# Seven block products for batch 1's second stage, and a ring of three places in the first two batches

## The chip, the cores and the metric

The kernel runs on one core of a Trainium2 chip. The metric is the device time of one execution in microseconds (us). The core has five engines with queues of their own: TensorE (PE) multiplies, VectorE (DVE) and ScalarE (ACT) work on tiles and empty PSUM, GpSimd (POOL) works on tiles in SBUF and issues transfers, SyncE (SP) issues transfers. The transfers of all queues run on the same 16 DMA engines.

## The reference

Eight batches, eight heads, 576 positions, head size 64. Attention looks back over a window of 128 positions with a bias that falls with the distance; its output is read as 4608 tokens of 512 numbers. They go through a layer that takes the largest of three products, and through an output product.

```python
scores = scale * np.matmul(q, k.transpose(0, 1, 3, 2))
mask = (rel >= 0) & (rel < window)
scores = np.where(mask, scores + bias[None], -1000000000.0)
...
attn = attn / (np.sum(attn, axis=-1, keepdims=True) + 1e-09)
x = np.matmul(attn, v)  # as (4608, 512)
h = np.maximum(np.maximum(x @ w1, x @ w2), x @ w3)   # (4608, 768)
out = h @ w_out                                      # (4608, 512)
```

## The kernel before

**Two stages a batch.** Each of the eight batches (`b`) has an attention part, 18 steps, and a part of two matmul stages. While the stages of batch `b` run, the attention steps of batch `b + 1` stand between their matmuls. The first stage has nine groups (`g`): three hidden parts `p` of 256 features times the three matrices w1, w2, w3. The second stage has two groups, for the output's features. Everything is kept transposed, so a group is a 2 × 2 block product: the weights of a group are four blocks e0 to e3, the activations four blocks by half of the features and half of the positions (288 columns). Every number is held as a high and a low part in the fp32r format, and one block product over 128 rows is three matmuls (low × high, high × low, high × high).

**Plain and seven products.** Batches 0 and 1 (`PB = 2`) run both stages plainly: `plain` (L763 holds the matmuls) makes four results of a group, each the sum of two block products. Batches 2 to 7 use `unit` (matmuls at L815): seven block products of sums and differences of the blocks (Strassen's scheme in Winograd's form). One of a first-stage group's seven is six matmuls, one of a second-stage group's is nine; a plain result is 12 in the first stage and 18 in the second. The seventh product of a group (k = 6) runs three places later, among the next group's. `factors_x` makes the seven factors of the activations, `factors_h` those of the hidden part: subtractions at L606 (`sub`), and cuts into high and low at L602 (ACT) and L603 (DVE). `plain_x` and `plain_h` make the four plain halves. Plain results leave PSUM at L774 (ACT) and L777 (DVE, the maximum), or at L703 for the output. Those of `unit` leave at L832 (ACT) and L705 to L722 (DVE). Three PSUM banks serve all of them in turn.

**Weights.** Batch 0 prepares the weights itself: `preparing` takes a group through four steps, `exponents` (L165 on DVE, for the last three groups L169 and L170 on ACT), `convert` (L176 or L180, then L185, all on DVE) with a store to `plain_keep` (L315), and two times `part`, which cuts blocks into high and low (L199 ACT, L202 DVE), stores them to `keep` (L212) and asks for the raw weights of the next but one group (`fetch`, L151). Raw weights have two slots. Each plain product of batch 0 takes one step. The seven block products need sums and differences of the weights' blocks as well: `more_sums` reads the plain blocks back (`load_sums`, L224, two groups at a time into the slots of the raw weights), POOL makes the sums (L194), `split_sums` cuts them (L199, L202), `store_sums` stores them to `keep` (L243, L244). Groups 0 to 8 are weights of the first stage, 9 to 11 of the second, which stay in the tile `ow`. The list of `more_sums` goes by `now`, a count of 77 for each batch, 63 of them for the first stage; a plain product of the first stage is 1.75 of it.

**The ring.** First-stage weights stand in a ring of two places of seven blocks. `stream` loads a group from `keep` in two pieces through POOL's queue (L351 in batch 1, L356 later) when `ahead` says that the place is free. A plain group uses four of a place's seven blocks.

```python
def ahead(n, a):
    ...
    i = ringed[a].index(n)
    return i < RING or (ringed[a][i - RING], 6 if a else 3) in used
```

**What sets the order.** The events of attention and products are sorted by a step number written out at the end of the kernel (`at`). This is the order of the program. The framework's planner may then change the order on an engine: by its own costs, it lets an instruction that is ready pass one that is not, earlier ones of the program first. From batch 2 on PE's order is kept as it is written, as is that of a few others (`keep_in_program_order`). At run time each engine and each queue works its list in order.

Of the kernel before, what the change touches and what calls it, by code (L numbers as in the profile page):

```python
# [27 lines left out]
RING = 2  # L28
# [8 lines left out]
def attention_maxout_kernel(  # L37
# [99 lines left out]
    ring = const.tile([P, RING, 7, 2, W], F32R, name="ring")  # L137
# [67 lines left out]

    def part(g, n):
        f = ring[:, g % RING] if g < 9 else ow[:, :, g - 9]
        k, e = (slice(5, 7), slice(2, 4)) if n else (slice(0, 5, 4), slice(0, 2))
        hi_lo(f[:, k, 0], f[:, k, 1], floats(g)[:, e])
        if g < 9:  # L210
            i, k = (3, slice(4, 7)) if n else (1, slice(0, 1))
            nc.sync.dma_start(keep[g][n][:, :i], f[:, k].bitcast(F32))  # L212
# [4 lines left out]
    def load_sums():  # L217
        nonlocal loaded
        r = raw_tile()
        for n in range(2):  # L220
            g = loaded
            loaded += 1
            ts[g] = t = r[:, 2 * DM * n:2 * DM * (n + 1)].rearrange("p (e w) -> p e w", e=4)
            nc.sync.dma_start(t.bitcast(F32), plain_keep[g])  # L224
            to_sum.extend((g, n, now + 8) for n in range(2))
# [21 lines left out]
    def more_sums():  # L247
        if loaded < NG and all(g in finished for g in range(loaded - 4, loaded - 2) if g >= 0):
            load_sums()
        if now < 63:  # L250
            return
        if to_split and now >= to_split[0][2] and (to_split[0][0] >= 9 or (9 + to_split[0][0], 1) in wts):
            g, a, _ = to_split.pop(0)
            split_sums(g, a)
            if a:
                if g < 9:
                    later(now + 3, store_sums, g)
                else:
                    finished.add(g)
        elif to_sum and now >= to_sum[0][2]:  # L260
            g, n, _ = to_sum.pop(0)
            sums(ts[g].bitcast(F32), n)
            if n:
                to_split.extend((g, a, max(now + 6, 77 * PB if a and g >= 9 else 0)) for a in range(2))
                to_split.sort(key=lambda x: x[2])

    def place(n, a):
        wts[n, a] = ring[:, ringed[a].index(n) % RING, 4 * a:7 - 3 * (1 - a)]
# [7 lines left out]
    def ahead(n, a):  # L276
        if (n, a) in SPARE:
            return begun == B and (n < LAST + 8 or made == B)
        i = ringed[a].index(n)
        return i < RING or (ringed[a][i - RING], 6 if a else 3) in used  # L280
# [60 lines left out]
    def stream():  # L341
        nonlocal streamed
        if streamed < len(stream_order) and prepared == 4 * NG and ahead(*stream_order[streamed]):
# [4 lines left out]
            if n < 9 * PB:  # L348
                place(n, a)
                e = 3 if a else 1  # L350
                nc.gpsimd.dma_start(wts[n, a][:, :e], keep[n % 9][a][:, :e])  # L351
                return
# [385 lines left out]
    def plain(b, v):  # L738
# [7 lines left out]
        j, i = divmod(r, 2)  # L746
        ps = ps_m.tile([P, 512], F32, name=f"ps_m{((PLAIN + 8) * b + v) % 3}")[:, :C]
        at = 9 * b + g
        if g < 9:
            if b == 0:  # L750
                weights(1.0, 4 * g_order.index(g) + 4)
            pairs = [
                (ring[:, at % RING, PLAIN_AT[h][i], a, kt * P:(kt + 1) * P], xs[b, h, j][:, c, kt])
# [24 lines left out]
        if w == 2:  # L778
            later(unit_of(b, v + 1), plain_h, b, p, (i, j))

    def unit(u):
# [6 lines left out]
        if n < 11 * PB or n >= 11 * B:  # L788
            return
# [33 lines left out]
        if b == PB and len(finished) < NG:  # L823
            more_sums()
# [49 lines left out]
    for b in range(PB):  # L874
        pace = (ready[b + 1] - when) / PLAIN
        for c in range(PLAIN + 8):
            if c == PLAIN:
                when = max(when, ready[b + 1])
                if b + 1 < PB:
                    at(when, plain_x, b + 1)  # L880
                else:
                    at(when, factors_x, b + 1, 77 * b + 63, 1.2)
            at(when, plain, b, c)
            when += pace if c < PLAIN else O_PACE * 14 / 8
# [71 lines left out]
```

## Time and profile before

| What | us |
|---|---|
| median of three runs | 757.75 |
| lowest and highest run | 757.32, 759.4 |
| profiled execution | 759.31 |
| its span, from the first to the last instruction | 757.6 |

The profile is one execution. Its rows give times from the start of the span. "Busy" is the time in which an engine had at least one instruction running; matmuls overlap, so a matmul's own duration is longer than the distance to the next one.

### The profile page before, as it was taken

The numbers are of one execution on the slowest core, as the hardware profiler recorded it, in microseconds if no ns is written. First come the engines' busy times: TensorE is split into PE (matmuls) and PEld (weight loads), VectorE is DVE, ScalarE is ACT, GpSimd is POOL, SyncE is SP. The second block draws the span as 40 slices with busy tenths as digits, with TensorE's granted clock in tenths as the row PEclk, the third lists the DMA queues.
The fourth block names the chain that finished last, engine by engine and source line by source line (L and its number), as shares of the span: only waits on it lengthen the run. The fifth ranks groups of instructions, "written<-read, shape, count | busy, mean of one in ns | idle before, by whom it ended". The sixth has DMA issues, their size and how long they took to land.

```text
span 757.6 us, 19290 instructions
## 1 busy us (share of the span) xinstructions
PE 736.8 (97%) x7216; PEld 676.0 (89%) x7221; DVE 516.2 (68%) x1617; ACT 482.4 (64%) x1597; POOL 235.9 (31%) x451
## 2 busy tenths in 40 slices
PE   7979999999999999999999999999999999999998
PEld 3448889998999999999999999999899999999998
DVE  4869977636559567794687657794777747683663
ACT  5775767666567767776766757676667767552342
POOL 4651214555555323222222123211222122333100
PEclk9999999999999999999999999999999999999999
DMA  7867999659999488864988479864988468789611
GB/s 250 302 234 262 326 334 336 214 199 288 308 330 386 146 271 305 280 209 153 329 295 288 135 245 306 304 217 144 300 283 276 166 221 285 269 252 367 235 65 63
DMA packets 57085, 192.81 MB, mean 254 GB/s; under 512 B 5792, under 2 KB 24480, under 8 KB 50464
## 3 DMA queue, kind: packets, MB, share of 16 engines
q0 software_dynamic: 20304, 108.54, 43.4%
q1 hardware_dynamic: 36400, 82.85, 31.3%
q8 instruction: 57, 0.93, 0.5%
q14 instruction: 36, 0.29, 0.1%
q10 hardware_dynamic: 288, 0.20, 0.1%
HBM read 156.95 MB, written 34.60 MB: 253 GB/s over the span
## 4 chain that ended last, share of the span: by engine, by line
PE 70%; DVE 10%; DMA 7%; POOL 5%; ACT 4%; issue 3%; SPq 0%; POOLq 0%; DVEq 0%; ACTq 0%
PE ps_m L815 45%; PE ps_m L763 11%; PE ps_s L420 4%; PE ps_x L555 4%; PE pt L488 4%; DMA ring<-keep 3%; DVE hs L603 2%; DMA hs<-in_w_all 2%; DVE hq L720 2%; DVE t L719 2%; POOL hs L194 2%; POOL pp L512 1%; POOL pp L508 1%; DMA keep<-hs 1%; DVE t L606 1%
## 5 line engine op out<-in xcount | busy, mean ns | idle before, releaser
L815 PE MATMUL ps_m<-xs,ring 128*128 128x288 f32 x2160 | 302.5, 297 | 1.8 <-DVE hq L722 1.3
L815 PEld LDWEIGHTS ps_m<-xs,ring 128*128 128x128 f32 x2160 | 290.1, 188 | 4.7 <-ACT t L832 3.1
L508 POOL TENSOR_SCALAR_AFFINE_SELECT pp<-pr 128x256 f32<-128x256 f32 x112 | 51.9, 463 | 278.3 <-ACT pr L492 152.9
L461 ACT ACTIVATE p<-s,st 128x128 f32<-128x128 f32 x288 | 114.6, 400 | 25.0 <-DVE st L449 20.8
L763 PE MATMUL ps_m<-xs,ring 128*128 128x288 f32 x864 | 123.1, 299 | 4.6 <-DMA ring<-keep 2.3
L763 PEld LDWEIGHTS ps_m<-xs,ring 128*128 128x128 f32 x864 | 116.3, 188 | 7.4 <-DMA ring<-keep 3.0
L832 ACT COPY t<-ps_m 128x288 f32<-128x288 f32 x196 | 76.8, 394 | 71.9 <-PE ps_m L815 69.9
L356 POOL DMA_DIRECT2D ring<-keep x103 | 55.5, 539 | 166.2 <-PE ps_m L815 155.6
L815 PE MATMUL ps_m<-hs,ow 128*128 128x288 f32 x756 | 105.7, 297 | 0.4
L815 PEld LDWEIGHTS ps_m<-hs,ow 128*128 128x128 f32 x756 | 100.9, 188 | 2.6 <-ACT t L832 1.2
L480 ACT ACTIVATE p<-p,st 128x128 f32<-128x128 f32 x252 | 84.8, 393 | 23.1 <-DVE st L468 23.1
L719 DVE TENSOR_TENSOR t<-ps_m,t 128x288 f32<-128x288 f32 x108 | 48.9, 453 | 43.6 <-PE ps_m L815 34.2
L449 DVE CUSTOM_DVE_ANT_0 s<-ps_s,bias 128x128 f32<-128x128 f32 x240 | 60.7, 285 | 11.1 <-POOL bias_t L111 4.6
L420 PE MATMUL ps_s<-qk 64*64 64x192 f32 (+1 forms) x1088 | 61.8, 319 | 1.5 <-DVE st L449 1.4
L602 ACT CAST hs<-hq 128x288 fp32r<-128x288 f32 x96 | 40.4, 432 | 34.3 <-DVE hq L720 17.8
L461 ACT ACTIVATION_READ_ACCUMULATOR p<-s,st 128x1 f32 x288 | 55.2, 192 | 0.0
L555 PE MATMUL ps_x<-pp,v 64*64 64x64 f32 (+3 forms) x1456 | 53.9, 276 | 0.0
L488 PE MATMUL pt<-plus,p 128*128 128x128 f32 x288 | 48.7, 287 | 3.6 <-POOL p L475 3.6
L555 PEld LDWEIGHTS ps_x<-pp,v 64*64 64x64 f32 x1456 | 42.3, 134 | 10.3 <-issue 9.2
L488 PEld LDWEIGHTS pt<-plus,p 128*128 128x128 f32 x288 | 30.5, 141 | 22.9 <-issue 12.9
L512 POOL TENSOR_SCALAR_AFFINE_SELECT pp<-pr 128x256 f32<-128x256 f32 (+1 forms) x112 | 50.3, 449 | 1.1
L589 DVE TENSOR_TENSOR xk<-ps_x,xk 128x256 f32<-128x256 f32 (+3 forms) x56 | 25.4, 454 | 36.8 <-ACT xk L588 36.8
(92 smaller groups left out, 954.4 us busy)
## 6 DMA issues: line engine op xcount, KB each, us to landing
ring<-keep POOLq DMA_DIRECT2D x51, 1024.0 KB, 7.3
ring<-keep POOLq DMA_DIRECT2D x61, 768.0 KB, 5.9
qk<-in_qk SPq DMA_DIRECT2D x31, 576.0 KB, 6.0
hs<-in_w_all SPq DMA_DIRECT2D x12, 1023.6 KB, 6.4
v<-in_v SPq DMA_DIRECT2D x32, 320.0 KB, 6.4
outT<-t SPq DMA_DIRECT2D x64, 144.0 KB, 1.8
keep<-ring SPq DMA_DIRECT2D x9, 768.0 KB, 6.0
plain<-hs SPq DMA_DIRECT2D x12, 512.0 KB, 4.2
```

Of the source, the lines that this page charges most:

```text
L420: pe(nc.tensor.matmul(ps[j][d:d + D, o:o + k1 - k0], lhsT=qkt[u][j * D:(j + 1) * D, 0, q0:q0 + D], rhs=qkt[u][j * D:(j + 1) * D, 1, k0:k1] ...
L449: nc.vector.tensor_tensor_reduce(out=x, in0=ps[j][:, P:2 * P], in1=below, scale=-0.125, scalar=3.0e38, op0=ALU.add, op1=ALU.min, accum_out ...
L461: nc.scalar.activation(p[:, j], x, AF.Exp, bias=st[:, 0, a, j:j + 1], scale=-1.0, accum_out=st[:, 1, a, j:j + 1])
L480: nc.scalar.activation(p[:, j], p[:, j], AF.Copy, scale=st[:, 2, a, j:j + 1])
L488: pe(nc.tensor.transpose(out=pt[:, a, j], in_=p[:, j], identity=ident))
L508: nc.gpsimd.affine_select(out=old, in_=src, pattern=[[-x, n] for x, n in pat], compare_op=ALU.is_gt, fill=0.0, base=0, channel_multiplier=1,)
L512: nc.gpsimd.affine_select(out=new, in_=low, pattern=pat, compare_op=ALU.is_ge, fill=0.0, base=0, channel_multiplier=-1,)
L555: pe(nc.tensor.matmul(x[j * D:(j + 1) * D, r, o:o + rhs.shape[1]], lhsT=vv[k, i, j * D:(j + 1) * D], rhs=rhs[k], start=start, stop=True, s ...
L719: nc.vector.tensor_tensor(out=s, in0=ps, in1=e, op=ALU.add)
L763: pe(nc.tensor.matmul(ps, lhsT=lt, rhs=rt, start=n == 0, stop=n == len(pairs) - 1, skip_group_check=True))
L815: pe(nc.tensor.matmul(part_of[n, {2: 0, 5: 0, 6: 0, 3: 1}.get(kk, kk)], lhsT=lt, rhs=rt, start=first, stop=i == len(pairs) - 1, skip_group ...
L832: nc.scalar.copy(out=e, in_=ps)
```

## The change

Batch 1's second stage goes through `unit` instead of `plain`, so the hidden part of batch 1 gets the seven factors, and the order of the four results of a group in batch 1 is that which `factors_h` expects. The ring becomes one row of 14 blocks; in batches 0 and 1 a group takes four of them, at one of three places, and later seven at one of two. `ahead` goes by the group three before instead of two before. The sums for the seven products must be done by batch 1's second stage, so the due times in `more_sums` are shorter, and a split and a sum may follow in one call.

```diff
-    ring = const.tile([P, RING, 7, 2, W], F32R, name="ring")
+    ring = const.tile([P, 7 * RING, 2, W], F32R, name="ring")
...
+    def plain_place(n):
+        return ring[:, 4 * (n % 3):4 * (n % 3) + 4]
...
     def part(g, n):
-        f = ring[:, g % RING] if g < 9 else ow[:, :, g - 9]
-        k, e = (slice(5, 7), slice(2, 4)) if n else (slice(0, 5, 4), slice(0, 2))
-        hi_lo(f[:, k, 0], f[:, k, 1], floats(g)[:, e])
+        e = slice(2 * n, 2 * n + 2)
         if g < 9:
-            i, k = (3, slice(4, 7)) if n else (1, slice(0, 1))
-            nc.sync.dma_start(keep[g][n][:, :i], f[:, k].bitcast(F32))
+            f = plain_place(g)
+            hi_lo(f[:, e, 0], f[:, e, 1], floats(g)[:, e])
+            k = slice(1, 4) if n else slice(0, 1)
+            nc.sync.dma_start(keep[g][n][:, :k.stop - k.start], f[:, k].bitcast(F32))
+        else:
+            f = ow[:, slice(5, 7) if n else slice(0, 5, 4), g - 9]
+            hi_lo(f[:, :, 0], f[:, :, 1], floats(g)[:, e])
...
-            to_sum.extend((g, n, now + 8) for n in range(2))
+            to_sum.extend((g, n, now + 7) for n in range(2))
...
-        if to_split and now >= to_split[0][2] and (to_split[0][0] >= 9 or (9 + to_split[0][0], 1) in wts):
+        if to_split and now >= to_split[0][2] and (to_split[0][0] >= 9 or streamed > 2 * to_split[0][0] + 1):
...
-                    later(now + 3, store_sums, g)
+                    later(now + 2, store_sums, g)
...
-        elif to_sum and now >= to_sum[0][2]:
+        if to_sum and now >= to_sum[0][2]:
...
-                to_split.extend((g, a, max(now + 6, 77 * PB if a and g >= 9 else 0)) for a in range(2))
+                to_split.extend((g, a, max(now + 4, 78 if a and g >= 9 else 0)) for a in range(2))
...
     def place(n, a):
-        wts[n, a] = ring[:, ringed[a].index(n) % RING, 4 * a:7 - 3 * (1 - a)]
+        k = 7 * (ringed[a].index(n) % RING)
+        wts[n, a] = ring[:, k + 4 * a:k + 7 - 3 * (1 - a)]
...
+        if n < 9 * PB:
+            return n < 3 or (n - 3, 3) in used
         i = ringed[a].index(n)
+        if i < 9 * PB + RING:
+            return all((x, 3) in used for x in range(i - 3, i - 1))
...
             if n < 9 * PB:
-                place(n, a)
-                e = 3 if a else 1
-                nc.gpsimd.dma_start(wts[n, a][:, :e], keep[n % 9][a][:, :e])
+                k = slice(1, 4) if a else slice(0, 1)
+                nc.gpsimd.dma_start(plain_place(n)[:, k], keep[n % 9][a][:, :k.stop - k.start])
                 return
...
-        j, i = divmod(r, 2)
+        j, i = ((0, 0), (0, 1), (1, 0), (1, 1))[r] if b < PB - 1 else ((1, 0), (0, 0), (1, 1), (0, 1))[r]
...
-        if w == 2:
+        if w == 2 and b < PB - 1:
             later(unit_of(b, v + 1), plain_h, b, p, (i, j))
+        elif w == 2:
+            factors_h(b, p, (i, j), unit_of(b, v + 1))
...
-        if n < 11 * PB or n >= 11 * B:
+        if n < 11 * PB - 2 or n >= 11 * B:
...
-        if b == PB and len(finished) < NG:
+        if len(finished) < NG:
             more_sums()
...
-            at(when, plain, b, c)
-            when += pace if c < PLAIN else O_PACE * 14 / 8
+            if c < PLAIN or b < PB - 1:
+                at(when, plain, b, c)
+                when += pace if c < PLAIN else O_PACE * 14 / 8
+        if b == PB - 1:
+            for u in range(77 * b + 63, 77 * b + 77):
+                at(when, unit, u)
+                when += O_PACE
```

## Rows read from the trace of the kernel before

**Rows 1.** The page, busy time, share and instructions of an engine.
```profile
PE 736.8 (97%) x7216; PEld 676.0 (89%) x7221; DVE 516.2 (68%) x1617; ACT 482.4 (64%) x1597; POOL 235.9 (31%) x451
```

**Rows 2.** Windows: stages of batches 0 and 1; length, busy by engine, clock, DMA.
```profile
core 0: us, PE busy (x) PEld busy (x) DVE busy (x) ACT busy (x) POOL busy (x), PEclk, DMA share, GB/s
58.64:139.36 80.72, 77.86 (x815) 71.67 (x815) 66.97 (x193) 54.48 (x171) 21.50 (x42) 0.98 0.89 319
139.36:161.03 21.67, 21.67 (x188) 20.86 (x185) 9.15 (x30) 12.84 (x43) 8.70 (x11) 1.00 0.52 174
161.03:238.13 77.10, 74.79 (x803) 70.62 (x802) 47.84 (x148) 50.17 (x165) 44.01 (x73) 1.00 0.93 306
238.13:260.56 22.43, 22.43 (x212) 21.62 (x210) 15.21 (x36) 15.61 (x47) 12.04 (x15) 1.00 0.65 232
```

**Rows 3.** Waits of PE, 58.64 to 260.56: us in total, times, longest.
```profile
PE ps_m L763 <- DMA ring<-keep: 2.3, 3, 1.4
PE ps_m L763 <- DVE hq L777: 1.9, 1, 1.9
PE ps_s L420 <- DVE st L449: 1.0, 1, 1.0
```

**Rows 4.** The chain of waits in batch 1: start, us, what.
```profile
169.47 8.81 DMA ring<-keep
...
195.10 9.44 DMA ring<-keep
...
206.07 8.15 DMA keep<-hs
214.28 5.02 DMA hs<-plain
...
222.61 7.58 DMA ring<-keep
```

**Rows 5.** The chain of waits in batch 0, 92 to 112.
```profile
93.35 7.07 DMA hs<-in_w_all
...
100.51 1.14 ACT hs L169
```

**Rows 6.** Windows: the stretch at the lower clock, columns as in rows 2.
```profile
108.93:112.35 3.42, 3.42 (x49) 2.56 (x47) 2.62 (x10) 3.30 (x11) 0.00 (x0) 0.50 0.98 397
```

**Rows 7.** Timeline of PE, batch 1's second stage, one of two such rows.
```profile
238.13 9.69 PE L763 MATMUL ps_m<-hs,ow 128*128 128x288 f32 x72
```

**Rows 8.** Lines L602, L603, L606, L705: duration ns min/median/max, first and last start.
```profile
L602 ACT CAST hs<-hq x96: 413/433/440, 76.5 to 740.5; 128x288 fp32r<-128x288 f32 x96
L603 DVE TENSOR_TENSOR hs<-hq,hs x96: 426/451/1079, 77.2 to 741.1; 128x288 fp32r<-128x288 f32 x96
L606 DVE TENSOR_TENSOR t<-hq,t x36: 445/451/455, 283.1 to 740.8; 128x288 f32<-128x288 f32 x36
L705 DVE TENSOR_TENSOR t<-ps_m,t x36: 441/457/459, 333.1 to 753.1; 128x288 f32<-128x288 f32 x36
```

**Rows 9.** Windows: batch 2's second stage, columns as in rows 2.
```profile
325.00:346.00 21.00, 20.94 (x198) 19.74 (x195) 16.90 (x51) 15.28 (x50) 3.32 (x7) 1.00 0.51 175
```

**Rows 10.** The sums and splits by line; last, L194 alone, windows added up.
```profile
L194 POOL TENSOR_TENSOR hs<-hs x48: 724/746/1417, 138.5 to 250.1; 128x256 f32<-128x256 f32 x48
...
L199 ACT CAST xs<-hs x18: 604/618/623, 147.3 to 232.2; 128x512 fp32r<-128x512 f32 x18
...
L202 DVE TENSOR_TENSOR hs<-hs,xs x18: 680/693/1249, 148.0 to 233.3; 128x512 fp32r<-128x512 f32 x18
...
161.00:238.00 77.00, 24.68 (x30) 1.00 0.93 305
238.00:260.50 22.50, 8.28 (x8) 1.00 0.65 234
```

**Rows 11.** Timeline of SP's issues in batch 0.
```profile
86.70 0.33 SPq L383 DMA_DIRECT2D qk<-in_qk  x1
87.14 0.43 SPq L315 DMA_DIRECT2D plain<-hs  x1
...
92.92 0.33 SPq L388 DMA_DIRECT2D v<-in_v  x1
93.35 0.38 SPq L151 DMA_DIRECT2D hs<-in_w_all  x1
```

More of the change, by code (lines that the diff above doesn't have):

```diff
@@ L752, in plain @@
             pairs = [
-                (ring[:, at % RING, PLAIN_AT[h][i], a, kt * P:(kt + 1) * P], xs[b, h, j][:, c, kt])
+                (plain_place(at)[:, (0, 3, 1, 2)[2 * h + i], a, kt * P:(kt + 1) * P], xs[b, h, j][:, c, kt])
                 for h in range(2) for kt in range(2) for a, c in ((0, 1), (1, 0), (0, 0))
```

## The prediction

> **What bounds the kernel now.** I read the page first: TensorE (PE) is busy 736.8 of 757.6 us [rows 1]. So time can come from fewer matmuls, from the 21 us in which PE is idle, or from a stretch at the lower clock. The stretches touched are batch 0 and batch 1, so I cut the span at their stages [rows 2]. Batch 0's first stage (58.64 to 139.36) holds 2.9 us of idle PE, batch 1's (161.03 to 238.13) 2.3 us, the two second stages none. The waits of PE name nearly all of that [rows 3]: three waits for a ring load (2.3 us together), one for VectorE's (DVE) maximum at L777 (1.9 us), one for a score (1.0 us).
>
> The chain of waits tells why the ring loads were late [rows 4]. The load issued at 169.47 took 8.81 us, the one at 195.10 took 9.44, the one at 222.61 7.58. With two places a group's load may start only when the group two before it is used up, so its whole lead is the four products of one group: (77.1 − 2.3) / 36 = 2.08 us each, 8.3 us. The DMA share there is 0.93 [rows 2], and no faster load is in sight.
>
> The wait for L777 comes from the preparation of weights in batch 0 [rows 5]: a load of raw weights issued at 93.35 lands 7.07 us later, ScalarE (ACT) has the exponents of that group next in its queue and starts them at 100.51, DVE's conversion waits for them, and the maximum that frees a PSUM bank stands behind the conversion on DVE. After that idle time the granted clock fell: 0.50 (1.2 GHz) from 108.93 to 112.35 with PE busy throughout [rows 6]. Half of 3.42 us, 1.7 us, is lost there, so this one late load cost 3.6 us.
>
> **The change part by part.** *Fewer block products.* Batch 1's second stage was two groups of four products of 18 matmuls, 144. It becomes two groups of seven of 9, 126 (the seventh of the last group runs among batch 2's first products, and is counted here). 72 such matmuls take 9.69 us [rows 7], 0.135 us each; 18 × 0.135 = **−2.4 us**. No matmul is added elsewhere, so I keep this as fixed.
>
> *Three places.* A place now comes free one group earlier, so a load in batch 1 has eight products, 16.6 us, before its use. The longest of the three took 9.44 [rows 4]; 7 us are left for a late issue. All three waits should go: **−2.3 us**, bounds −2.3 and 0. The loads keep their size and their number; one issue of some 0.55 us stands per half group, on the same POOL queue. The first three groups of batch 1 are now loaded within batch 0, into a second stage where DMA is busy 0.52 [rows 2]. The page DMA: Bandwidth & Descriptors of the Trainium skill (Anatomy of one DMA) gives 2.0 us plus bytes at 436 GB/s, an estimate of 3.8 us for these 768 KB. By that a lead of 8.3 us would be ample, the third place would bring nothing and the sum would be −2.4; the rows, twice as long, contradict it.
>
> *Batch 2's first two groups* still enter the ring when groups 16 and 17 of the plain places are used: the same products as before, nothing gained or lost.
>
> *Factors instead of plain halves.* Each of the three hidden parts now needs seven cuts instead of four and four subtractions. In all 9 more casts on ACT (0.433 us, 3.9 us), 9 more low parts (0.451) and 12 subtractions (0.451) on DVE, 9.5 us. The outputs: six DVE additions (0.457) come in, 2.7 us, and ACT keeps about eight copies [rows 8]. So DVE gets 12.2 us more, ACT 3.9. What hides it: DVE is busy 47.8 of 77.1 us in the first stage and 15.2 of 22.4 in the second [rows 2]. Some 5.9 us of it belongs to the second stage (3 low parts, 4 subtractions, 6 additions at 0.45). The nearest like stretch is batch 2's second stage, 325 to 346: the same seven products with the same factors of the next batch, DVE 16.9 of 21 us, PE 20.94 [rows 9]. That cover held, so I cost it at **0**. Bounds 0 and +3, half of the 5.9 us laid bare; a gain is excluded, since PE is not idle there.
>
> *Sums moved forward.* The twelve groups' sums (48 POOL instructions, 0.746 us median), their splits (ACT 0.618, DVE 0.693) and stores all have to end before batch 1's second stage. Working through the code's list by its due times: the pairs of loads were asked for at products 2, 11, 19 and 28 of batch 1 and are now at 1, 7, 15 and 23; the last splits, before in batch 2, are now at products 31 to 34. Work and bytes are the same, only packed. Does the last pair come in time? Before, the pair asked for at product 19 (161.0 + 19 × 2.14 = 201.7) was issued at 214.28, behind a store that took 8.15 us, and its load took 5.02 [rows 4], 17.6 us after asking (219.3). Now the last pair is asked for at 161.0 + 23 × 2.08 = 208.8, and so lands near 226.4. Its eight POOL sums at 0.87 (24.68 + 8.28 us for 30 + 8 of them [rows 10]) bring 233.3, the last split, cast and low part one after the other, about 2 us more: 235.3. The second stage begins at 238.13 − 2.3 = 235.8, and its second block product meets the last group's factors 15 matmuls later, near 237.8. The margin is 2.5 us: **0**, bounds 0 and +5 (one more block like the store's 8.15 us, less the margin and rounded). What queues behind a late load: on POOL the masks of the attention and the ring issues; on SP the stores and the loads of q, k and v. Before, SP stood still for the 8 us of that store without a wait of PE but the ring's [rows 3, 4].
>
> *POOL beside DVE.* The same instruction of POOL takes from 0.724 to 1.417 us, the DVE subtraction of the split 0.680 to 1.249 [rows 10]. The page GPSIMD Engine Reference of the Trainium skill (Key points) says that POOL shares its way into SBUF with DVE and suffers from DVE instructions with two inputs there; these rows agree. At 1.417 eight sums take 11.3 us instead of 6.9, and the margin of 2.5 us is gone: this is the third rival's mechanism.
>
> *Preparation moved forward.* Group n's parts used to wait for group n − 2's use, now n − 3's; in the order of the code each step comes three products earlier in batch 0. But the trace shows these steps held by the raw loads, whose slot has to be stored first, not by the ring. So they can hardly run earlier. What changes is SP's order. Before, a store waited behind a q,k load (86.70, 87.14) and the raw load behind a v load (92.92, 93.35) [rows 11]. By their places in the code both now go ahead, which I estimate at one to two us on the load that came late. Against it, the planner may now put exponents still further ahead of PSUM evictions. Bounds −3.6 (the stall and its clock go) and +3.6 (one more of the kind). Both ends are equally far, so I take **0**.
>
> **Sum.** −2.4 − 2.3 + 0 + 0 + 0 = −4.7 us. The profiled execution took 759.31 us with a span of 757.6, 0.2% above the median of the runs, 757.75. I take the difference off the median: **753.0 us**.
>
> **The rivals.**
> 1. *The preparation's stall goes too.* For it: SP's new order. Against: the raw loads themselves take 7 us in a stretch with DMA at 0.89 [rows 2]. −4.7 − 3.6: 749.4.
> 2. *The third place brings nothing*, since the DMA engines are full (0.93) and an earlier issue only makes each load slower. −2.4: 755.4. Against it: each load gets 8.3 us more of lead, and the stretch before has room (0.52).
> 3. *The last sums come late* and the second stage waits, with POOL slowed by DVE or SP blocked once more by 8 us: +2 to +5 on the forecast, 755 to 758. It decides from a delay of 2.5 us on.
> 4. *Slower:* exponents placed three products further ahead of evictions make ACT and DVE wait for raw loads that arrive when they always did, PE runs out of PSUM banks. Each such stall costs 1.9 + 1.7 us as seen once [rows 3, 6]. One gives 756.6; from two on (7.2 us) the change loses: 760.2. For it: DVE is the busiest there, 67.0 of 80.7 us. Against: the steps already ran later than their places in the code ask.
>
> **How the numbers follow.** Chances: forecast 0.42, rival 1 0.20, rival 2 0.10, rival 3 0.15, rival 4 0.13. A measurement of this kernel can tell some 0.3%, 2.3 us, from no change, so the border lies at 755.5. Faster: forecast, rival 1, half of rival 2 and a third of rival 3 less a bit for the unseen, 0.69. Slower: half of rival 4 and what mishaps I did not see, 0.11. Same: the rest, 0.20. The range reaches down past rival 1 (749.4, and one microsecond more if the score's wait [rows 3] goes as well) and up to rival 3's end and past one stall of rival 4: 748.4 to 758.0. What is left out is two stalls, and less than 2 in 10.
>
> **What would show each step.** 126 instead of 144 matmuls on hidden and output weights in batch 1, and its two stages shorter by 2.4 us beside the waits. No PE wait for a ring load in batch 1, with the loads still 7 to 9 us long but issued a group ahead. DVE at about 0.8 in batch 1's second stage with PE without idle time. POOL's last sum some 2 us before that stage begins. In batch 0 one clock drop after one idle stretch, as before, or none (rival 1), or two (rival 4). I am wrong if PE idles at the head of batch 1's second stage, or if batch 0's first stage changes by more than 2 us.

## The result and the profile after

The changed kernel is slower, by about 1%: 768.04 us (median of 8 runs, 765.31 to 770.77) beside 760.79 us for the kernel before (8 runs on the same chip, 757.32 to 764.59). The ratio is 1.0098, 95% interval 1.0073 to 1.0124. The forecast was 753.0 us, with 748.4 to 758.0 as the range and 0.11 as the chance of slower. The profiled execution took 767.95 us, its span is 766.2.

The page of the changed kernel, for [rows 1]:

```profile
PE 739.0 (96%) x7198; PEld 675.9 (88%) x7203; DVE 525.8 (69%) x1644; ACT 483.8 (63%) x1606; POOL 234.7 (31%) x451
```

The 18 matmuls are gone (7216 to 7198), and yet PE is busy 2.2 us longer, part of it at half clock. DVE has 9.6 us more, ACT 1.4. Windows of the same stages, columns as in [rows 2]; the last line is both batch 1's second and batch 2's first stage, and two short windows follow in a second answer:

```profile
60.66:142.17 81.51, 77.70 (x815) 70.51 (x815) 67.43 (x193) 54.83 (x171) 23.57 (x44) 1.00 0.90 326
142.17:163.84 21.67, 21.67 (x188) 20.86 (x185) 10.83 (x31) 13.30 (x44) 14.16 (x17) 1.00 0.64 220
163.84:244.97 81.13, 76.03 (x803) 71.89 (x802) 55.03 (x162) 52.43 (x173) 45.23 (x74) 0.98 0.86 287
244.97:332.77 87.80, 84.60 (x837) 79.98 (x839) 59.53 (x200) 58.54 (x201) 20.21 (x45) 0.98 0.71 238
...
221.30:224.70 3.40, 3.20 (x15) 2.92 (x15) 3.40 (x12) 2.44 (x10) 1.48 (x3) 0.50 0.98 324
252.00:255.40 3.40, 3.40 (x16) 3.40 (x16) 2.30 (x4) 2.74 (x9) 0.00 (x0) 0.50 0.00 0
```

Batch 0, from the first line's start to the second's end, lasts as long as before within a microsecond (103.18 and 102.39 us). Batch 1's first stage takes 81.13 us instead of 77.10, with 5.1 us of idle PE instead of 2.3 and 3.4 us at half clock. Here DVE is busy 55.0 us instead of 47.8. Another idle stretch and another 3.4 us at half clock stand in the second stage. The 2.0 us by which the window begins later (60.66 against 58.64) arise in the first 22 us: PE waits 1.6 us for a load of q and k there, and the clock stands at 0.50 for 6.8 us instead of 3.4. They are no mark of the change: in the nine profiles of kernels with the changed kernel's batch 0, this point lies between 57.7 and 61.0, and the kernel before's among them. PE's waits of the changed kernel, for [rows 3]:

```profile
PE ps_m L773 <- DVE hq L787: 4.3, 3, 3.8
PE ps_m L827 <- ACT t L844: 3.1, 1, 3.1
PE ps_m L773 <- ACT hq L784: 1.3, 1, 1.3
```

No ring load is waited for in batch 1's first stage any more. What PE waits for are PSUM banks: DVE's maximum (L787), ACT's copies out of PSUM (L784, L844). The chain of waits of the changed kernel, for [rows 4], says who was late before 221:

```profile
189.94 7.00 DMA ring<-keep
...
197.34 3.91 DMA keep<-hs
...
201.68 5.86 DMA hs<-plain
207.54 0.95 POOL hs L194
...
211.00 5.85 DMA ring<-keep
...
221.08 0.38 DVE hq L787
```

One round trip: a ring load, the store of sums that may overwrite its source only after it (SP waits), the load of the next groups' blocks behind that store on SP's queue, the sums on POOL. The timeline shows what stood behind it, ACT first, then DVE:

```profile
213.65 0.62 ACT L199 CAST xs<-hs 128x512 fp32r<-128x512 f32 x1 [5.38 <-POOL hs L194]
214.18 0.43 ACT L612 CAST hs<-hq 128x288 fp32r<-128x288 f32 x1
...
214.63 0.80 DVE L613 TENSOR_TENSOR hs<-hq,hs 128x288 fp32r<-128x288 f32 x1 [4.58 <-ACT hs L612]
...
221.00 0.45 DVE L787 TENSOR_TENSOR hq<-ps_m,hq 128x288 f32<-128x288 f32 x1
```

A split of sums (L199) held ACT for 5.38 us. The cut of a hidden factor (L612) is next in ACT's list, and DVE waited 4.58 us for it. Then everything that had piled up ran first, until at 221.00 the maximum came for which PE had stood since 217.7. (L202, L613 and L616 are DVE's low parts and differences; in this pile of 6.4 us they were stretched by about 1.2 us, so the 4.58 us of waiting weigh more.)

### The profile page after: what moved, and what is told of

Its sections match the earlier page's. It is cut to its first block, busy times and chain, and to the rows that moved or that the text cites. A ratio compares the mean times of both kernels' runs of the same rounds, so it can differ in the third digit from the quotient of the medians.

```text
span 766.2 us, 19305 instructions
## 1 busy us (share of the span) xinstructions
PE 739.0 (96%) x7198; PEld 675.9 (88%) x7203; DVE 525.8 (69%) x1644; ACT 483.8 (63%) x1606; POOL 234.7 (31%) x451
## 4 chain that ended last, share of the span: by engine, by line
PE 68%; DVE 11%; DMA 8%; ACT 6%; POOL 3%; issue 3%; SPq 0%; POOLq 0%; DVEq 0%; ACTq 0%
PE ps_m L827 46%; PE ps_m L773 9%; DMA ring<-keep 4%; PE ps_s L430 4%; PE pt L498 4%; PE ps_x L565 4%; DVE hs L613 2%; ACT p L471 2%; DVE hq L730 2%; DVE t L729 2%; DMA qk<-in_qk 1%; POOL pp L522 1%; POOL p L485 1%; DMA keep<-hs 1%; ACT p L490 1%
## 5 line engine op out<-in xcount | busy, mean ns | idle before, releaser
L518 POOL TENSOR_SCALAR_AFFINE_SELECT pp<-pr 128x256 f32<-128x256 f32 x112 | 53.0, 474 | 291.7 <-ACT pr L502 160.1
L827 PE MATMUL ps_m<-hs,ow 128*128 128x288 f32 x882 | 124.9, 299 | 3.5 <-ACT t L844 3.1
L844 ACT COPY t<-ps_m 128x288 f32<-128x288 f32 x202 | 78.9, 393 | 72.9 <-PE ps_m L827 71.0
L827 PEld LDWEIGHTS ps_m<-hs,ow 128*128 128x128 f32 x882 | 119.4, 190 | 5.9 <-ACT t L844 4.5
L612 ACT CAST hs<-hq 128x288 fp32r<-128x288 f32 x96 | 40.2, 433 | 26.9 <-DVE hq L730 17.8
L522 POOL TENSOR_SCALAR_AFFINE_SELECT pp<-pr 128x256 f32<-128x256 f32 (+1 forms) x112 | 50.1, 448 | 1.1
```

The lines of the kernel that those rows point to most:

```text
L522: nc.gpsimd.affine_select(out=new, in_=low, pattern=pat, compare_op=ALU.is_ge, fill=0.0, base=0, channel_multiplier=-1,)
L827: pe(nc.tensor.matmul(part_of[n, {2: 0, 5: 0, 6: 0, 3: 1}.get(kk, kk)], lhsT=lt, rhs=rt, start=first, stop=i == len(pairs) - 1, skip_group ...
L844: nc.scalar.copy(out=e, in_=ps)
```

## The experiments

Three theories were put up. **Theory 1**: the sums, due earlier, make ACT and DVE stand behind late loads and late POOL sums. **Theory 2**: the factors' extra work on DVE and ACT starves PE of PSUM banks. **Theory 3**: the third place itself does harm. Each run is compared with the kernel before on its own chip.

### Three places alone

The change without its second stage and with the old due times:

```diff
-            to_sum.extend((g, n, now + 7) for n in range(2))
+            to_sum.extend((g, n, now + 8) for n in range(2))
...
-        if n < 11 * PB - 2 or n >= 11 * B:
+        if n < 11 * PB or n >= 11 * B:
```

> Three places of four blocks, but batch 1's second stage plain and the due times of the sums as in the kernel before. Theory 1 (the sums' earlier due times make ACT and DVE stand behind late POOL sums): the three ring waits of 2.3 us go and nothing else comes, ratio to the kernel before 0.995 to 0.998. Theory 2 (the 12 us more of DVE work for the seven factors are what starves PE of PSUM banks): the same, 0.995 to 0.998. Theory 3 (the third place itself harms, by earlier preparation in batch 0 or by earlier ring loads): 1.003 or more, with new idle stretches of PE in the two first stages.

Measured 757.28 us (12 runs), ratio **0.9956** (0.9931 to 0.9981): faster than both kernels, and theory 3 falls. Its windows (batch 1's first stage, then all up to the end of batch 2's first stage), and the shares of its chain of waits between 160 and 236:

```profile
163.03:237.04 74.01, 74.01 (x803) 70.55 (x801) 46.67 (x145) 49.66 (x165) 43.83 (x73) 1.00 0.94 318
237.04:322.25 85.21, 85.07 (x855) 80.70 (x856) 60.00 (x191) 59.51 (x202) 27.70 (x52) 1.00 0.74 251
```

```profile
by line: PE ps_m L773 78.2%; PE ps_x L565 8.5%; PE ps_s L430 7.2%; PE pt L498 6.2%
```

PE has no idle time in 74 us, no DMA is left in the chain, and the DMA share is still 0.94. ACT's splits wait for POOL's sums here too, 6.2 us in four pieces of at most 2.7, without a cost to PE.

### Three places and early sums

The same with the changed kernel's due times; the second stage stays plain.

> As e1, but with the changed kernel's due times of the sums (load to sum 7, sum to split 4, split to store 2, a split and a sum in one call); batch 1's second stage plain, no factors of the hidden part. Theory 1: the idle stretches of batch 1's first stage (3.8 and 1.3 us, and 1.7 us of clock) are there without any factor: 6.8 less 2.3 won, ratio 1.004 to 1.007. Theory 2: they are not there, 0.995 to 0.999.

Measured 760.78 us (12 runs), ratio 0.999 (0.9967 to 1.0014). The early sums alone cost 3.5 us (757.28 to 760.78): less than theory 1 expected, and the upper end of what theory 2 allowed. Its first stage in the windows, and ACT's waits in it:

```profile
162.47:240.70 78.23, 75.11 (x804) 70.68 (x801) 47.38 (x145) 48.48 (x161) 44.76 (x74) 1.00 0.92 297
```

```profile
ACT ow L199 <- POOL hs L194: 8.0, 2, 4.9
```

4.2 us more than with the old due times at nearly the same busy time of DVE and ACT: it isn't work but waiting. PE's waits show behind what:

```profile
PE ps_x L565 <- POOL pp L518: 1.3, 1, 1.3
PE ps_m L773 <- DVE hq L787: 1.2, 2, 0.6
PE ps_x L565 <- POOL pp L522: 0.7, 1, 0.7
```

Of the 3.1 us of idle PE, 2.0 stand before products that need the attention's masks (L518, L522): on POOL these came behind six sums in a row (211.3 to 216.6), after POOL had stood 6.0 us for the load they read. The other 1.2 us are maxima on DVE (at 233.8 and 236.3) behind a low part (L202) whose split ACT had held for 4.9 us. So late sums stop two lists, POOL's own and ACT's.

### No sums on POOL

The changed kernel without the 48 sums, so that what is cut and stored from batch 1 on are unsummed blocks.

```diff
-            sums(ts[g].bitcast(F32), n)
             if n:
```

> The changed kernel with the 48 sums on POOL left out (loads, splits and stores stay, so the seven products use plain blocks in place of sums). Theory 1: ACT's casts no longer wait for POOL, the idle stretches of batch 1's first stage go (5.1 us and 1.7 us of clock), the 3.1 us at the second stage stay: ratio to the kernel before about 1.001. Theory 2: no change from the changed kernel, 1.008 to 1.011.

Measured 764.16 us (10 runs), ratio 1.0057 (1.0033 to 1.0082). Less loss, but the stall stayed: between what the two theories expected (1.001; 1.008 to 1.011). In its profile, taken from the slowest of its runs (768.87), PE is idle 6.0 us at 213.3. ACT now waits for the transfers themselves:

```profile
ACT xs L611 <- DMA keep<-xs: 5.5, 1, 5.5
ACT xs L199 <- DMA hs<-plain: 4.8, 1, 4.8
```

The first is a cut that needs a slot whose sums are still on their way out, the second a split whose load is late. POOL's sums are one link of the round trip; without them the late transfers alone make a stall.

### A tile of its own for the fourth block

```diff
+            if n:
+                nc.sync.dma_start(last_keep[g], f[:, 3:4].bitcast(F32))
...
```

> The changed kernel, but the plain fourth block of a group is kept in a DRAM tile of its own, so that the store of the fourth sum does not wait on SP for the ring load that reads the plain fourth block from the same place. One more store and one more ring issue of 256 KB per group, the same bytes. Theory 1, with SP's waits for ring loads as the start of the chain: those waits of SP go, the sums' loads land some 4 us earlier against the products, the 3.8 us idle stretch shrinks below 1: 1.001 to 1.004. Theory 2: no change, 1.008 to 1.011. If the sums are late for another reason than that wait: no change either, with SP's waits gone.

Measured 767.95 us (6 runs), ratio 1.0095 (1.0062 to 1.0128): no gain, where theory 1 had 1.001 to 1.004. SP's waits for ring loads in batch 1 (28.0 us in the changed kernel) are gone, and SP waits for its own stores instead, in front of the next load:

```profile
SPq L233 <- DMA keep<-hs: 25.9, 8, 8.2
```

### Four cuts instead of seven factors

The factors behind batch 1's first stage are not formed; products 1, 2 and 6 of its second stage read the cuts of 0, 3 and 4. 12 differences and 9 cuts are left out.

```diff
     def factors_h(b, p, ij, when):
+        if b == PB - 1 and p < 3:
+            return four_h(b, p, ij, when)
```

> The changed kernel, but behind each three first-stage blocks of batch 1 the seven factors are not formed: only the four maxima are cut (as in the kernel before), and products 1, 2 and 6 read the cuts of products 0, 3 and 4, so the values of batch 1 are not the reference's. All matmuls, waits for weights, sums and due times stay; 12 differences and 9 cuts (about 9.5 us of VectorE, 3.9 us of ScalarE) are gone. Theory 2 (the factors' work starves TensorE of banks): the idle of 3.8 us near 217 and the one of 3.1 us in the second stage go, batch 1's first stage takes 76 to 78, the second about 20; ratio 0.994 to 1.000. Theory 1 (the sums, early and behind a long DMA round trip, stop ScalarE's queue): the first stage keeps an idle of 2 us or more and takes 79 to 81, only the second stage's idle goes; ratio 1.002 to 1.006.

Measured 763.55 us (11 runs), ratio 1.0043 (1.0017 to 1.0069), as theory 1 expected. PE's waits:

```profile
PE ps_m L800 <- DVE hq L814: 4.1, 2, 3.9
PE ps_m L854 <- ACT t L871: 1.4, 2, 1.2
```

The stall near 217 needs no factors: 3.9 us, as before. The one in the second stage falls from 3.1 to 1.2 us, and no clock drop follows it.

### Four cuts for the last third only

The same with `p == 2` in place of `p < 3`.

> As the run with four cuts, but only for the last third of batch 1's inner rows (p = 2), whose factors are formed at the seam of its two stages; the factors of p = 0 and 1 stay. Leaves out 4 differences and 3 cuts (3.2 us of VectorE, 1.3 of ScalarE) right before the second stage. If the second stage's idle of 3.1 us comes from those factors, it is under 1 us here and the second stage takes 20.5 to 21.5 with no clock drop behind it; the first stage keeps its idle near 217 under both theories. Ratio 1.002 to 1.006. If it comes from the next batch's factors instead, idle stays at 2.5 to 3 us and the ratio at 1.008 to 1.010.

Measured 765.18 us (11 runs), ratio 1.0067 (1.0041 to 1.0093). The second stage's idle was 2.2 us, between what the two readings expected, so the last third's factors look like a part of it. The first stage's long idle now stood at 195.9 (2.5 us) instead of 217.7.

### The next batch's factors later

```diff
-                    at(when, factors_x, b + 1, 77 * b + 63, 1.2)
+                    at(when, factors_x, b + 1, 77 * b + 68, 1.2)
```

> The changed kernel with the seven input factors of batch 2 begun five units later in batch 1's second stage (about 7 us), so that they don't stand among the last factors of batch 1; nothing is left out. If the idle of 3.1 us at 247.6 is VectorE's pile of both batches' factors, it falls under 1.5 us and the clock drop behind it goes: ratio 1.003 to 1.007. If the last factors of batch 1 alone do it, nothing changes there (1.008 to 1.011); if batch 2's first unit then waits for its factors, an idle of 1 to 3 us shows at the start of batch 2 instead.

Measured 765.23 us (11 runs), ratio 1.0048 (1.0026 to 1.0071). The time is in the expected range, but not for the reason given: the idle in the second stage was 2.6 us, hardly less; no clock drop followed it in the profile.

### No sums, and a tile of its own

Both links of the round trip out, all factors kept (unsummed blocks, as above).

> The changed kernel without the 48 sums on GpSimd (the folded weights stay plain sums' inputs, so the values from batch 1's second stage on are not the reference's) and with the fourth plain block in a tile of its own, so that SyncE's stores of sums don't wait for the ring's loads. Loads, splits and stores of the sums stay. Theory 1 (what stops ScalarE is a split that waits for its load and sum): with both links of the round trip out, the splits find their data there, the first stage has no idle over 1.5 us and takes 77 to 78; ratio 0.998 to 1.003. Theory 2 (factors): idle of 3 to 4 us near 217 stays; ratio 1.005 to 1.010.

Measured 760.34 us (11 runs), ratio 0.9995 (0.997 to 1.0019). The first stage takes 78.1 us, 2.3 us of it idle at 214.8, where theory 1 had under 1.5. Most of the loss is gone, not all.

### No sums, a tile of its own, and four cuts

> The changed kernel with both suspects out: four cuts instead of seven factors (12 differences and 9 cuts left out), no sums on GpSimd, and the fourth plain block in a tile of its own. The values from batch 1's second stage on are not the reference's; all matmuls, ring loads, splits and stores of sums stay. If these two causes are all of the loss, what is left is the run with three places alone (0.9956) less 18 matmuls (2.4 us of 761, 0.0032): ratio 0.990 to 0.995, first stage 74 to 75.5, second 20.1 to 20.6, no idle over 1 us. If something else in the change costs (the blocks' order in the first stage, the order of loads), ratio 0.997 to 1.002 with idle over 2 us somewhere in batch 1.

Measured 757.62 us (11 runs), ratio 0.9963 (0.9938 to 0.9989), between the two readings (0.990 to 0.995 and 0.997 to 1.002). Its windows:

```profile
166.58:241.88 75.30, 74.26 (x803) 70.57 (x802) 47.15 (x152) 51.04 (x169) 23.18 (x48) 1.00 0.93 306
241.88:325.34 83.46, 83.14 (x837) 78.47 (x838) 55.55 (x189) 56.47 (x196) 20.14 (x45) 1.00 0.73 250
```

With both suspects out the first stage has one idle stretch of 1.0 us, the second stage none that counts. Here the 18 fewer matmuls can be read: 83.46 against 85.21 us with three places alone, PE busy 83.14 against 85.07. Yet the whole is no faster than three places alone (0.9956), which still makes all the sums: the first stage is 1.3 us longer (75.30 against 74.01). What costs that, if it is more than noise, is not shown: the order of a group's four results and the early due times of the splits are still the changed ones, and no run takes either back alone.

### A tile of its own and four cuts, sums kept

> The changed kernel with four cuts instead of seven factors behind batch 1's first stage (12 differences and 9 cuts left out, so batch 1's values are not the reference's) and the fourth plain block in a tile of its own; sums on GpSimd kept. It is the fourth cell beside own block (1.0095), own block without sums (0.9995) and own block without sums and with four cuts (0.9963). If sums and factors add up, the idle of batch 1's first stage is 1.5 to 3 us and the ratio 1.002 to 1.006. If the loss needs both at once, idle under 1.2 us and 0.995 to 0.999.

Measured 762.65 us (11 runs), ratio 1.002 (0.9995 to 1.0046), as expected if the two add up, with 3.3 us of idle in the first stage (1.5 to 3 were expected). With the earlier runs this closes a table, all with the fourth block in a tile of its own (ratios to the kernel before, intervals above):

| | sums on POOL | no sums on POOL |
|---|---|---|
| seven factors | 1.0095 | 0.9995 |
| four cuts | 1.0020 | 0.9963 |

The sums cost 0.0100 beside seven factors and 0.0057 beside four cuts; the factors 0.0075 beside the sums and 0.0032 without. Each costs by itself; whether they cost more together is open (0.0043, with intervals of about 0.003 to either side on each cell).

### The factors' work, for nothing

Three places alone (plain second stage), with 4 differences and 3 cuts into scratch tiles for each third of batch 1's hidden part. The result is not touched. First with the old due times of the sums, then with the early ones.

```diff
+        for k in range(4 if ij == (1, 1) else 0):
+            later(when + k + 1, sub, t, hq[p, ij], hq[p, (0, 0)])
+        if ij != (0, 0):
+            later(when + 1, cut)
```

> The run with three places alone (plain second stage, old pace of the sums), with the work that seven factors add put in as work for nothing: behind the blocks of each third of batch 1's first stage 4 differences and 3 cuts into scratch tiles, 12 and 9 in all, 9.5 us of VectorE and 3.9 of ScalarE. The output is not changed by it. My prediction had this work at 0: ratio 0.994 to 0.998, no idle over 1 us in batch 1's first stage. If VectorE, slowed beside GpSimd's sums, can't take it, idle of 1.5 us or more there and a ratio of 0.998 to 1.004.

Measured 760.78 us (11 runs), ratio 0.9997 (0.9972 to 1.0023): 0.0041 more than three places alone, and 2.3 us of idle in the first stage that wasn't there, before products that waited for ACT's copies out of PSUM. The work is not free even at the old pace.

> The same work for nothing, with the sums at the changed kernel's early pace; still 18 plain products a block in batch 1's second stage, so what is left of the change is only its load on the other engines. If that load is the whole loss (no product, no order of blocks), the first stage shows idle of 3 to 5 us near 197 and 217 as in the changed kernel, and the ratio is 1.004 to 1.010 (18 matmuls more than the changed kernel). If the loss needs the seven products' own order and waits, ratio 0.999 to 1.003.

Measured 763.33 us (11 runs), ratio 1.0039 (1.001 to 1.0068). The first stages of both:

```profile
160.98:237.77 76.79, 74.54 (x804) 70.61 (x802) 51.95 (x160) 50.94 (x171) 43.72 (x73) 1.00 0.91 305
```

```profile
164.27:247.56 83.29, 75.62 (x804) 70.72 (x802) 57.55 (x159) 50.56 (x168) 45.41 (x74) 1.00 0.84 279
```

The second has the same work as the first, DVE busy 5.6 us longer with it, and 7.7 us of idle PE (idle stretches of 2.9 us at 198.0 and 2.4 at 238.8 among them), without any of the seven products. Its profiled execution was the slowest of its runs (768.07), so only the kind of idle, not its sum, is to be read from it.

### More slack for the sums

Three attempts to keep the seven products and loosen the rest, all with the fourth block's own tile; nothing is left out. First: sums from 52 of `now` on, 9 units behind the load, splits 7 behind the sum.

```diff
-        if now < 63:
+        if now < 52:
...
-            to_sum.extend((g, n, now + 7) for n in range(2))
+            to_sum.extend((g, n, now + 9) for n in range(2))
```

> The changed kernel with the fourth plain block in a tile of its own, so that splits and stores of sums need not follow the ring's loads, with the sums begun at unit 52 instead of 63, and each given more time: due 9 units behind its load (before 7), its split 7 units behind the sum (before 4). Nothing is left out. Theory 1 (ScalarE stands behind a split whose load and sum are late): the split at about 212 finds its sum done, the first stage's idle near 217 falls from 3.8 to under 1.5 us, and with it the clock drop goes; first stage 76.5 to 78.5; the second stage's idle of about 3 us stays; ratio 1.000 to 1.004. Theory 2 (factors' work): idle of 3 us or more near 217 stays, ratio 1.007 to 1.010.

Measured 765.4 us (5 runs), ratio 1.0061 (1.0038 to 1.0084). The idle at 215.6 fell from 3.8 to 2.3 us, but one of 2.0 came at 226.5; the ratio lies between the two theories' (1.000 to 1.004 and 1.007 to 1.010). Second, with the next batch's factors later as well:

> As the run with slack for the sums, and the input factors of batch 2 begun five units later in batch 1's second stage. If both causes named so far are all of the loss: no idle over 1.5 us in the first stage, 1 to 2.5 us in the second; ratio 0.996 to 1.001. If the factors' own work costs on, ratio 1.003 to 1.007.

Measured 764.11 us (8 runs), ratio 1.0038 (1.0018 to 1.0058): the best of the versions with seven products that leave nothing out, and slower than the kernel before. It is in the range that stood for "the factors' own work costs on". Third, with sums from 63 on, 8 and 6 units:

> As the run with slack and late factors, but the sums begin at unit 63 as in the changed kernel, due 8 units behind the load and the split 6 behind the sum. Nothing is left out. Tells whether beginning earlier matters or only the slack of each: theory 1 expects the idle near 217 under 1.5 us as well and a ratio of 0.996 to 1.002; theory 2 3 us or more and 1.003 to 1.007.

Measured 769.04 us (5 runs), ratio 1.01 (1.0077 to 1.0123): a split stood 4.7 us for a POOL sum, and PE was idle 5.6 us at 197.1. None of these due times removes the stall, they move it about.

The second of these shows what is left when the sums are hardly late (ACT waits for them at most 1.4 us). Its timeline, DVE and then POOL (L618 and L621 are the cut's low part and the difference there, L195 the sums):

```profile
208.75 2.05 DVE L618 TENSOR_TENSOR hs<-t,hs 128x288 fp32r<-128x288 f32 x1
210.73 0.45 DVE L792 TENSOR_TENSOR hq<-ps_m,hq 128x288 f32<-128x288 f32 x1
...
211.87 0.99 DVE L621 TENSOR_TENSOR t<-hq,t 128x288 f32<-128x288 f32 x1
212.78 0.99 DVE L621 TENSOR_TENSOR hq<-hq 128x288 f32<-128x288 f32 x1
...
209.05 4.41 POOL L195 TENSOR_TENSOR hs<-hs 128x256 f32<-128x256 f32 x5
```

While POOL makes its sums, a difference takes 0.99 us and a low part 2.05 instead of 0.45. DVE runs without a gap, and PE waits for the maximum behind it.

## Why the prediction was wrong

The change was forecast at −4.7 us and measured at +7.25. Another 3.0 us of the miss lie in the base: 757.75 was the median of three runs, and eight gave 760.79.

**Right: the ring.** "−2.3 us, all three waits should go" was borne out: none is left in the changed kernel, and three places alone gain 3.4 us (0.0044 of 760.67), the largest part of it batch 1's first stage at 74.0 instead of 77.1 us. By the estimate of 3.8 us from the Trainium skill's page DMA: Bandwidth & Descriptors (Anatomy of one DMA) the third place would have brought nothing; the run decides against that estimate, as [rows 4] had.

**Right in kind, too large: the matmuls.** 18 × 0.135 = 2.4 us; 1.9 us of busy PE (85.07 − 83.14) and 1.75 us of time were measured. Why it isn't 2.4 stays open.

**Failed: "Sums moved forward: 0".** I asked only whether the last pair comes before the second stage needs it. It does: POOL's last sum ended at 237.2, 7.8 us before that stage. I listed what queues behind a late load on POOL (the masks) and SP and gave it no price, on the strength of the kernel before, where PE hadn't waited for it; with the early sums alone PE waits 2.0 us for those masks. Not listed was ACT: a split stands in its list like any other instruction, and the cuts of the hidden part and the copies out of PSUM stand behind it. The splits follow their sums 4 units later instead of 6, which would catch them unready; three distances were shortened at once, and no run separates them. Measured: 3.5 us (three places, early against old due times), inside the bound of +5 but by another mechanism than the late last pair.

**Failed: "Factors: 0".** The cover that I took as proof, batch 2's second stage [rows 9], has 3.3 us of POOL in 21; batch 1's first stage has 45 in 81. I let the mean busy time of DVE (47.8 of 77.1) stand for the room in it and bounded only the second stage's 5.9 us. Durations came from the median of all batches [rows 8]. In the changed kernel the longest took three to four and a half times the median (lines; duration in ns, shortest, median, longest):

```profile
L613 DVE TENSOR_TENSOR hs<-t,hs x63: 440/450/2036, 187.1 to 750.7; 128x288 fp32r<-128x288 f32 x63
...
L616 DVE TENSOR_TENSOR hq<-hq x21: 443/448/1373, 190.2 to 747.4; 128x288 f32<-128x288 f32 x21
...
L787 DVE TENSOR_TENSOR hq<-ps_m,hq x48: 420/449/458, 69.7 to 247.0; 128x288 f32<-128x288 f32 x48
```

Without the sums on POOL the same two groups read:

```profile
L612 DVE TENSOR_TENSOR hs<-t,hs x63: 443/452/649, 187.6 to 751.6; 128x288 fp32r<-128x288 f32 x63
...
L615 DVE TENSOR_TENSOR hq<-hq x21: 444/451/453, 189.9 to 748.3; 128x288 f32<-128x288 f32 x21
```

The effect in one place of the changed kernel, DVE and then POOL:

```profile
191.52 2.04 DVE L613 TENSOR_TENSOR hs<-t,hs 128x288 fp32r<-128x288 f32 x1
193.59 0.87 DVE L616 TENSOR_TENSOR t<-hq,t 128x288 f32<-128x288 f32 x1
...
191.81 2.35 POOL L194 TENSOR_TENSOR hs<-hs 128x256 f32<-128x256 f32 x3
```

These two and the two differences before them (from 189.40) took 5.18 us. Without the sums the same four took 1.78 (from 189.60), and PE's idle of 1.3 us, which follows at 197.5 in the changed kernel, isn't there.

The maxima, which read one operand from PSUM, are not slowed (0.458 us at most); the factors, which read both from SBUF, are. The Trainium skill's page SBUF — State Buffer (SBUF: two separate sides) says that a DVE instruction with two SBUF inputs and a POOL instruction that reads SBUF exclude each other for whole instructions. The trace agrees with it; the prediction used such a rule only for the sums' own duration. Measured cost of the factors' work by itself: 3.1 us (0.0041 of 760.67, a difference of two ratios each known to about 0.0025). How much of it is the stretching and how much the bare work isn't shown; without the sums the factors cost 0.0032.

**How they add up.** Against three places alone: early sums +0.0034, extra work +0.0041, both +0.0083, so within the intervals they add. The changed kernel lies another 0.0059, 4.5 us, above that, though it has 18 matmuls less. So with their 1.75 us some 6.2 us are to be accounted for. What its profile has there and the run with the work for nothing doesn't is the second stage's wait, 3.1 us, and the clock drop behind it, 1.7 us. The remaining 1.4 us are open; the intervals are wider than that. DVE and ACT carry their backlog over the seam, and the copies (L844) that free the banks come late. Here nothing is stretched: the last sum has ended, a factor takes its 0.45 us, and DVE has no gap above 0.2 us from 240.7 to 253. ACT's waits of the changed kernel between 240 and 253:

```profile
ACT hs L612 <- DVE t L616: 2.1, 2, 1.1
```

Which of the works at the seam makes it is not settled: leaving out the last third's factors took 0.8 us off, moving the next batch's 0.5, leaving out all three thirds' 1.9, the sums (with a tile of its own) 2.1, and only all together the whole.

**Priced in one place only: the clock.** Rival 4 and the bounds of batch 0's preparation added 1.7 us of clock to a stall; the bounds of the two terms in batch 1, +3 and +5, did not. In the profile of the changed kernel the clock costs 2 × 1.7 us there, behind the two longest stalls. The mean granted clock over the eight runs was 0.990, over the runs of three places alone 0.995, as for the kernel before beside it; half a percent of 760 us is about 4 us. That is no measure of the stalls alone: in the profiles the half clock of the first 20 us and of batch 0 also differs from one execution to the next.

**The rivals.** The third (last sums late) named the neighbourhood, not the mechanism. The fourth, with 0.13, had it: ACT and DVE wait for a transfer that arrives when it does, PE runs out of banks, the clock falls, and from two such stalls on the change loses. I looked for it in batch 0's preparation, and the same sentence was due for the sums in batch 1. Batch 0 did not change by more than a microsecond: the 1.9 us wait of [rows 3] went, and small waits for banks and masks came, 3.8 us of idle against 2.9. The sign "PE idles at the head of batch 1's second stage" came true, 2.6 us into it, but PE stood there for ACT's copies and not for a late factor of the weights.

## What to carry to other kernels

Before moving work forward, list for each engine that works its list in order what stands right behind each moved instruction, and whether PE needs that; a split that waits 5 us for a sum costs PE the bank that a cheap copy behind it would have freed. Cover must be read in the stretch where the work will run, with the same neighbours: here DVE had 30 us of room on paper, and beside POOL's sums four short instructions took 5.18 us instead of 1.78. When a change has a part that pays by itself (three places, 0.9956), measure that part alone before tying it to another.

## What was unexpected of the hardware

- A DVE difference or low part with both operands in SBUF took up to 2.04 us instead of 0.45 beside POOL's sums; the maximum with one operand in PSUM at most 0.458.
- In batch 1 of all these profiles, 9 of the 11 idle stretches of PE of 2.5 us or more were followed by 3.4 or 6.8 us at a granted clock of 0.50 (1.2 GHz), and 4 of the 10 between 2.0 and 2.5 us. The length of one idle stretch doesn't decide it alone: in batch 0 all sixteen profiles with three places have waits of 0.4 and 0.9 us near 118, and in six of them 3.4 us at 0.50 follow. The stall of 3.8 us cost about 5.5 with its clock; the two of 2.3 and 2.0 us in the version with slack and late factors cost no clock at all.
- A tile of its own for the fourth block took SP's 28.0 us of waits for ring loads away and gave 25.9 us of waits for its own stores instead: what SP waited for changed, hardly how long (58 us in all against 62, 160 to 250).
